# A three-engine attention and Fourier kernel: new chunk order, later values, filter products on GpSimd, one PSUM tile

## The chip, the cores and the metric

The kernel runs on one core of a Trainium2 chip. The metric is the device time of one execution in microseconds, with the median over the runs. Engines are named as the profile names them: PE (TensorE), ACT (ScalarE), DVE (VectorE), POOL (GpSimd), SP (SyncE, which issues DMAs).

## What is computed

The input x has 2048 rows of 448 values. The result is a gated mix of two branches: softmax attention with 16 heads of 28 values, and a spectral filter (a two-dimensional real FFT, a product with a complex weight, and the inverse).

```python
g = sigmoid((x * gate_w).sum(-1, keepdims=True))
qkv = (x @ wqkv) -> q, k, v            # 16 heads of 28
a = softmax(q @ k.T / sqrt(28)) @ v @ wo
X = rfft2(x.astype(float32)) * (w_r + 1j * w_i)
b = irfft2(X, s=(2048, 448)).astype(bfloat16)
return g * a + (1 - g) * b
```

## The kernel before

**Work.** The 16 heads are taken in four groups G of four. A group has four query blocks j of 512 queries; one group and one block make a chunk, 16 in all. A chunk has 16 packs, one for each block of 128 keys, and a pack has four scores tiles of 128 keys x 512 queries, one per head. That is 256 packs.

**Two ways to an exponential.** A pack goes one of two ways. On ACT, two of its score tiles at a time lie side by side in a PSUM tile of two banks and one ACTIVATE (line 862) makes the exponentials of 128 x 1024 scores. On DVE the exponential is put together from integer arithmetic: line 891 turns the scores of one head into bits (128 x 512, out of PSUM), and line 897 makes three shifted copies of the whole pack (128 x 2048, SBUF to SBUF); four variants are then summed by PE. In before 200 packs go to ACT (400 ACTIVATEs) and 56 to DVE (224 of line 891, 168 of line 897).

**PE.** All matmuls are issued from line 913. A score matmul uses 32 rows of the array, so that up to four heads can run side by side. Values (psV) use four tiles of 32 columns side by side; projections and the Fourier matmuls as well (`mmc`, line 915).

**PSUM.** Eight banks of 128 x 512 f32. In before they are six tiles: psA and psB with two banks each for the score tiles of ACT, three tiles psX0 to psX2 of one bank each for everything that DVE evicts (its scores, projections, Fourier steps, output), and psV with one bank for the sum over keys.

```python
self.psS = [ps.tile([128, n, 512], F32, name=f"ps{'AB'[i]}") for i, n in enumerate(sizes)]
self.psX = [ps.tile([128, 512], F32, name=f"psX{i}") for i in range(len(CFG["xbanks"]))]
self.psV = ps.tile([128, 512], F32, name="psV")
```

**Order.** The kernel writes its order of instructions itself. `Plan` (lines 158 to 824) holds an estimated duration for each operation, due times for each piece of side work (`unit(at, name, due)`), and weights (`CFG`, lines 827 to 833). It plays the engines forward and notes in which order every engine takes its work; `build` then emits the instructions in that order, and each engine executes its own list in order. The plan knows banks ("A0", "A1", "B0", "B1", "X0" to "X2", "V") and when each is free. The waits between engines are not the plan's: the framework puts them in when the instructions are emitted, from the tiles that each reads and writes.

**Side work.** Projections of keys and queries (`proj`), of values (`values`, 16 units of 449 columns with all 16 heads and the gate's logit), the forward transform (`fft1`, `fft2`), the product with the filter (line 1384, DVE, out of PSUM), sums of the products on GpSimd (line 1391), the inverse transform (`fft2`, `fft3`), normalising each chunk (`norms`, through small DMAs), and the output (`final`, 16 blocks of 128 rows).

Of the kernel before, what the change touches and what calls it, by code (L numbers as in the profile page):

```python
# [18 lines left out]
FP = F + 1  # L19
# [8 lines left out]
BITS_MIN = 256.0  # L28

# [128 lines left out]
class Plan:  # L158
# [3 lines left out]
    def __init__(self, cfg):  # L162
        self.cfg = cfg
        self.out = []
        self.avail = {e: [] for e in ("ACT", "DVE", "POOL", "SP")}
        self.T = {e: 0.7 for e in ("PE", "ACT", "DVE", "POOL", "SP")}
        self.units = []
        self.ops = []
        self.seq = 0
        self.npend = 0  # L170
# [102 lines left out]
    def run(self):  # L273
# [18 lines left out]
        limit = 1200.0  # L292
        while self.npend > 0 or not self.stream_over():
            eng = min(self.T, key=self.T.get)
            t = self.T[eng]
            if t > limit:
                raise RuntimeError("the plan does not end: " + self.state())
            ok = self.pe_step(t) if eng == "PE" else self.step(eng, t)
            if not ok:
                self.T[eng] = t + 0.02  # L300
# [44 lines left out]
    def setup_stream(self, q_ready, k_ready, v_ready, emit):  # L345
# [14 lines left out]
        self.bank_of = [[f"{'AB'[i]}{k}" for k in range(n)] for i, n in enumerate(self.sizes)]  # L360
        self.last_exp = [None] * len(self.sizes)
# [32 lines left out]
    def operands(self, p):  # L394

        ci, kt = divmod(p, 16)
        a, b = self.q_ready[ci], self.k_ready[ci // 4][kt // 4]
        if a.end is None or b.end is None:
            return None
        return max(a.end, b.end)  # L400
# [9 lines left out]
    def next_tile(self):  # L410
# [7 lines left out]
        while len(units) < size:  # L418
            if cur is None:
# [31 lines left out]
        self.tile = dict(k=k, units=units, ready=ready, slots=slots, grp=k % len(self.sizes))  # L451
        self.ntile += 1
        return self.tile

# [38 lines left out]
    def exp_run(self, e, t):  # L493
# [4 lines left out]
        e["end"] = o.end  # L498
        if not any(self.s_left) and self.last_exp[e["grp"]] is e:
# [5 lines left out]
        for p, h in e["units"]:  # L505
            a = self.act_pack[p]
            a["exps"].append(o)
            if len(a["exps"]) == 4:
                ci, kt = divmod(p, 16)
                x = Op("PE", 0, None, [self.v_ready[ci // 4][kt]] + a["exps"], name="pv")  # L510
# [47 lines left out]
    def d_run(self, d, h, bank, t, conc):  # L558
# [19 lines left out]
        self.s_mark(d["p"] // 64, o.end)  # L578
# [3 lines left out]
    def d_sums(self, d):  # L582
        p = d["p"]
        ci, kt = divmod(p, 16)
        vr = self.v_ready[ci // 4][kt]
# [34 lines left out]
    def pe_step(self, t):  # L620
# [35 lines left out]
        pool = c["xbanks"] if (self.started or self.reserve) and any(self.s_left) else self.allb  # L656
# [67 lines left out]
    def s_run(self, tl, t):  # L724
        self.started = True
        u = Op("PE", 0, None, [], name="s")
# [5 lines left out]
        for b in self.bank_of[tl["grp"]]:  # L732
            self.owner[b] = "stream"
# [4 lines left out]
        for p, h in tl["units"]:  # L738
            G = p // 64
# [5 lines left out]
        fb = self.free_banks(t, self.cfg["xbanks"])  # L745
# [82 lines left out]
    tiles=(2, 2), xbanks=("X0", "X1", "X2"), nring=20, nvar=10, nearly=5, l_pe=0.09, l_act=0.03, pe_lat=0.20,  # L828
    dma_issue=0.6, m_pe=0.2, m_bank=0.1, tol=0.15, max_ahead=9, nd_max=99, d_open=3, ahead=3, d_chunks=1,
    dve_op1=0.605, dve_shift=0.60, pool_shift=2.0, pool_shifts=(), pool_every=0, prio_op1=3, prio_shift=3, sh_max=4, d_urg=0,  # L830
    window=3.413, z_hard=3250, z_soft=3500,
    w_pv=1.0, w_open=0.5, w_new=1.6, w_late=0.5, w_d=3, w_due=2, hungry=1.4, v_rush=0.5, x_rush=4.0, k_rush=5.0, q_rush=0.0, w_hungry=1, sw_pen=0, pv_min=1, ring_urg=2, d_first=True,
# [3 lines left out]
class Emit:  # L836
# [5 lines left out]
    def score(self, p, h, bank):  # L842
        k = self.k
        ci, kt = divmod(p, 16)
        G, j = divmod(ci, 4)
# [3 lines left out]
    def scores(self, tl):  # L849
        for i, (p, h) in enumerate(tl["units"]):  # L850
            self.score(p, h, self.k.pl.bank_ap(f"{'AB'[tl['grp']]}{i}"))

    def exp(self, e):
# [8 lines left out]
        k.nc.scalar.activation(out=out, in_=k.psS[e["grp"]][:, 0:n, :], func=ACT.Exp, scale=LN2_128)  # L862
# [10 lines left out]
    def value(self, p, h, rhs, x):  # L873
        k = self.k
        ci, kt = divmod(p, 16)
        G = ci // 4
# [27 lines left out]
class Kernel:  # L904
# [27 lines left out]
    def tiles(self, ctx):  # L932
# [7 lines left out]
        sizes = CFG["tiles"]  # L940
        self.psS = [ps.tile([128, n, 512], F32, name=f"ps{'AB'[i]}") for i, n in enumerate(sizes)]
        self.psX = [ps.tile([128, 512], F32, name=f"psX{i}") for i in range(len(CFG["xbanks"]))]
# [37 lines left out]
        self.Wo = sb("Wo", [128, NG, D])  # L980
# [4 lines left out]
        self.t12 = [[sb(f"t{n}{i}", [128, 2 * FP]) for n in (1, 2)] for i in range(2)]  # L985
        self.P = sb("P", [128, CFG["nring"], 512])
# [25 lines left out]
    def plan(self):  # L1012
        pl = self.pl = Plan(CFG)
        pl.banks = {}
        for i, n in enumerate(CFG["tiles"]):
            for k in range(n):
                pl.banks[f"{'AB'[i]}{k}"] = self.psS[i][:, k, :]
        for i, b in enumerate(CFG["xbanks"]):
            pl.banks[b] = self.psX[i][:, :]
# [12 lines left out]
        self.group(1, 1.0)  # L1032
        self.gate()
        self.fft2()
        self.group(2, 4.3)
        self.group(3, 8.3)
# [23 lines left out]
    def loads(self):  # L1060
# [10 lines left out]
        self.d_wv = self.dma(self.Wv[0:C, :, 0:D], w3[:, :, 2 * D:3 * D], 9.4, **fast)  # L1071
        self.d_gw = self.dma(self.Wv[0:C, :, D:D + 1], self.gw.rearrange("(c k o) -> k c o", c=NC, o=1), 9.4)
# [21 lines left out]
        self.m_wo = pl.op("POOL", 1.9, lambda e: nc.gpsimd.memset(self.Wo[:, :, :], 0.0), prio=6, port=True)  # L1094
        self.d_wo = []
        wov = self.wo.rearrange("(g h d) n -> h d g n", g=NG, h=4)
        for h in range(4):
            self.d_wo.append(self.dma(self.Wo[32 * h + 1:32 * h + 29, :, :], wov[h], 3.0, [self.m_wo, self.d_bi], prio=7))
# [31 lines left out]
    def square(self, eng, src, i, deps, prio=4, alt=None):  # L1130
# [9 lines left out]
    def head(self):  # L1140
        pl, nc = self.pl, self.nc
        self.o_xT = [[] for _ in range(4)]
        for b in range(4):
            for cp in range(2):
                u = pl.unit(-10, "xT", due=-1, rush=6.0 if b == 0 else CFG["x_rush"])
# [24 lines left out]
        u = pl.unit(-8, "w", due=-1, rush=6.0)  # L1170
# [10 lines left out]
        self.m_wo.deps.append(self.o_wt)  # L1181
        self.queries(0, -6.9945, None, [1, 2, 3], "DVE", deps=[self.o_wt])

    def first(self, which, b, name, sel, one):
# [3 lines left out]
        u = self.proj((-9.5 if b == 0 else -9.0) + 0.1 * b, which, 0, b, name, due=-1, rush=6.0 if b == 0 else CFG["k_rush"])  # L1188
# [13 lines left out]
    def queries(self, G, at, nk, blocks, eng, deps=(), alt=None, span=0.0):  # L1202
# [3 lines left out]
        due = at + 1.5 if G else 0.3  # L1206
# [38 lines left out]
    def group(self, G, at, span=0.18):  # L1245
# [3 lines left out]
        for b in range(4):  # L1249
            u = self.proj(at + span * b, 0, G, b, "k", deps=free, due=at + 1.2)  # L1250
            self.k_ready[G][b] = self.ev_k(u, G, b, deps=free)
            sqs.append(self.square("POOL", self.KT[G % 2][:, 512 * b:512 * b + 512], b, [self.k_ready[G][b], self.sq_use[b]]))
        u = pl.unit(at + span * 4, "kn", due=at + 1.3)
# [12 lines left out]
        u = pl.unit(at + span * 4, "kb", due=at + 1.3)  # L1266
        u.mm(lambda bank: self.mm(bank[:, 0:1], self.mrow4[:, :, :].rearrange("p b h -> p (b h)"), self.one[0:1, 1:2], True, True), n=60, kind="row", deps=[b2])
        nk = u.use("DVE", 0.1, lambda bank, e: nc.vector.tensor_copy(out=self.nks[G % 2][:, :], in_=bank[:, 0:1]), prio=2)
        self.queries(G, at + span * 5, nk, [0, 1, 2, 3], "POOL", deps=free, span=span)


    def values(self):
        nc = self.nc
        self.o_g, evs = [], []
        for t in range(NT):
            u = self.pl.unit(-7 + 0.001 * t, "v", due=(t + 2) / 16, rush=CFG["v_rush"])
            b = t // 4
            for c in range(NC):
                u.mm(lambda bank, c=c, t=t: self.mmc(bank[:, 0:449], self.xT[0:C, c, 128 * t:128 * t + 128], self.Wv[0:C, c, :], c == 0, c == NC - 1),
                     n=449, kind="bg", eff=0.875, deps=self.o_xT[b] + [self.d_wv, self.d_gw])  # L1280

            def ev(bank, e, t=t):
                out = self.Vb[:, t, :, 1:29]
                in_ = bank[:, 0:448].rearrange("p (h d) -> p h d", d=DH)
                nc.scalar.copy(out=out, in_=in_) if e == "ACT" else nc.vector.tensor_copy(out=out, in_=in_)
            o = u.use("DVE", dict(DVE=0.54, ACT=0.5), ev, deps=[self.m_v1], alt="ACT", prio=2)
            evs.append(o)
            for G in range(1, NG):
                self.v_ready[G][t] = o
            self.o_g.append(u.use("DVE", 0.09, lambda bank, e, t=t: nc.vector.tensor_copy(out=self.glog[:, t:t + 1], in_=bank[:, 448:449]), prio=2))  # L1290
        for b in range(4):
# [4 lines left out]
            o = self.pl.op("DVE", dict(DVE=0.54, POOL=1.0), weigh, evs[4 * b:4 * b + 4] + [self.o_wt], prio=0, port=True)  # L1296
            for t in range(4 * b, 4 * b + 4):
                self.v_ready[0][t] = o

    def gate(self):  # L1300
        pl, nc = self.pl, self.nc
        a = pl.op("ACT", 0.12, lambda e: nc.scalar.activation(out=self.ge[:, :], in_=self.glog[:, :], func=ACT.Exp, scale=-1.0), self.o_g)
        a = pl.op("DVE", 0.1, lambda e: nc.vector.tensor_scalar_add(out=self.ge[:, :], in0=self.ge[:, :], scalar1=1.0), [a], port=True)
        a = pl.op("DVE", 0.25, lambda e: nc.vector.reciprocal(out=self.ge[:, :], in_=self.ge[:, :]), [a])
        a = pl.op("DVE", 0.1, lambda e: nc.vector.tensor_copy(out=self.gg[:, 0, :], in_=self.ge[:, :]), [a], port=True)
        a = pl.op("DVE", 0.1, lambda e: nc.vector.tensor_scalar(out=self.gg[:, 1, :], in0=self.gg[:, 0, :], scalar1=-1.0, scalar2=1.0, op0=ALU.mult, op1=ALU.add), [a], port=True)
        u = pl.unit(0.0, "gT", due=0.9)
        u.mm(lambda bank: nc.tensor.transpose(out=bank.bitcast(BF16)[0:32, 0:128], in_=self.gg[:, :, :].rearrange("p a t -> p (a t)"), identity=self.ident), n=128, deps=[a])
        a = u.use("DVE", 0.2, lambda bank, e: nc.vector.tensor_copy(out=self.grow[:, :], in_=bank.bitcast(BF16)[0:32, 0:128]))
        d = self.dma(self.gd[:, :], self.grow[:, :], 2.1, [a])  # L1310
        g = self.gd[:, :]
        self.d_gq = [self.dma(self.gq[32 * h:32 * h + 32, :, :], raw_ap(g, [[16, 32], [512, 4], [1, 16]]), 2.3, [d]) for h in range(4)]
# [46 lines left out]
    def fft2(self):  # L1359
        nc, pl = self.nc, self.pl  # L1360
        loads = [self.load_g(0, [self.d_bd]), self.load_g(1, [self.d_bd])]
        p2use, tuse = [None, None], [[], []]
# [181 lines left out]
```

## Time and profile before

| | us |
|---|---|
| median of 3 runs | 418.14 (417.87 to 425.62) |
| the profiled execution | 417.98 |
| its span | 416.2 |
| first exponential of ACT starts at | 17.39 |
| last one starts at | 399.25 |
| GpSimd busy | 102.4 |

The span is the time from the first to the last instruction that the profile shows; the profiled execution's own time is 1.8 us longer. In a group's row stand the line, the engine, what is written and read, the count, then busy time, the mean duration in ns, and the idle time of the engine ahead of these instructions with what ended it. A timeline row begins with the start and the time it covers, both in us. "PEclk" is the granted clock of TensorE as a share of full speed. A duration in the profile includes the way through the engine: two ACTIVATEs that follow each other without a wait overlap for about 0.1 us.

### The profile page before, as it was taken

How to read it: one execution, taken by the hardware profiler on the slowest of the kernel's cores; microseconds unless marked ns; L12 is line 12 of the kernel's file. 1: busy time of each engine (PE TensorE's matmuls, PEld its weight loads, DVE VectorE, ACT ScalarE, POOL GpSimd, SP SyncE). 2: the span in 40 equal slices, each digit the busy share in tenths (PEclk: the TensorE clock that was granted, in tenths of full speed). 3: DMA queues.
4: the chain of work that ended last, by engine and by line, in shares of the span. 5: the costliest groups of instructions: out<-in, count | busy, mean ns of one | idle time of the engine just before them, and what ended most of it. 6: DMA issues, size and time to landing. Idle time of an engine off the chain costs nothing.

```text
span 416.2 us, 12278 instructions
## 1 busy us (share of the span) xinstructions
PE 394.5 (95%) x5030; PEld 136.2 (33%) x5030; DVE 367.7 (88%) x677; ACT 382.4 (92%) x418; POOL 102.4 (25%) x144
## 2 busy tenths in 40 slices
PE   7999999999999999999999999999999999999993
PEld 4433343222333323323333223223333322223251
DVE  3547699999999999989999899899998999999991
ACT  3895989999999999999999999999999989999941
POOL 0251102652221323331302242251367111010100
PEclk9999999999999999999999999999999989999998
DMA  8520001221022202021121201100100100010203
GB/s 263 151 62 7 4 2 17 53 41 39 11 57 52 84 8 63 4 64 32 37 74 46 58 8 59 39 28 4 28 3 2 28 2 27 4 50 4 70 8 106
DMA packets 23929, 17.66 MB, mean 42 GB/s; under 512 B 15268, under 2 KB 19281, under 8 KB 23873
## 3 DMA queue, kind: packets, MB, share of 16 engines
q1 hardware_dynamic: 22800, 16.59, 14.8%
q8 instruction: 39, 0.64, 0.7%
q10 hardware_dynamic: 1072, 0.29, 0.3%
q14 instruction: 18, 0.14, 0.1%
HBM read 14.71 MB, written 1.97 MB: 40 GB/s over the span
## 4 chain that ended last, share of the span: by engine, by line
PE 42%; ACT 25%; DVE 16%; issue 6%; DMA 6%; SPq 2%; ACTq 0%; DVEq 0%; POOL 0%
ACT P L862 25%; PE psX L913 15%; PE psV L913 13%; PE psB L913 7%; PE psA L913 7%; DVE VS L897 5%; DVE VS L891 5%; DMA rs<-osb 3%; DMA Qf<-in_A_wqkv_dram 2%; SPq L1055 2%; DMA out_dram<-ost 2%; DVE osb L1449 1%; DVE t L1384 1%; DVE tab L1426 1%; DVE QT L1220 0%
## 5 line engine op out<-in xcount | busy, mean ns | idle before, releaser
L862 ACT ACTIVATE P<-psA 128x1024 bf16<-128x1024 f32 x195 | 205.9, 1056 | 7.7 <-PE psV L913 5.4
L862 ACT ACTIVATE P<-psB 128x1024 bf16<-128x1024 f32 x195 | 206.0, 1056 | 3.3 <-PE psB L913 2.1
L891 DVE TENSOR_SCALAR VS<-psX 128x512 int16<-128x512 f32 x224 | 145.4, 680 | 6.1 <-PE psX L913 5.5
L897 DVE TENSOR_SCALAR VS<-VS 128x2048 int16<-128x2048 int16 x168 | 111.1, 714 | 0.4
L913 PEld LDWEIGHTS <-KT 32*128 32x128 bf16 (+1 forms) x1040 | 46.0, 91 | 144.4 <-issue 141.4
L913 PE MATMUL psV<-VS,Vb 128*32 128x512 bf16 x916 | 82.2, 389 | 2.0 <-DVE VS L897 1.7
L913 PE MATMUL psB<-QT,KT 32*128 32x512 bf16 x400 | 78.4, 384 | 5.9 <-ACT P L862 5.0
L913 PE MATMUL psA<-QT,KT 32*128 32x512 bf16 x400 | 79.7, 384 | 1.1 <-ACT P L862 0.6
L913 PE MATMUL psV<-P,Vb 128*32 128x512 bf16 x780 | 74.6, 386 | 0.0
L913 PE MATMUL psX<-QT,KT 32*128 32x512 bf16 x224 | 73.1, 384 | 1.3 <-DVE VS L891 0.6
L913 PEld LDWEIGHTS <-Vb 128*32 128x32 bf16 x1696 | 36.7, 94 | 64.8 <-issue 59.1
L1391 POOL TENSOR_TENSOR t<-t,t 128x226 bf16<-128x226 bf16 x32 | 19.1, 618 | 59.2 <-DVE t L1384 49.9
L1137 POOL TENSOR_TENSOR sq<-QT 128x512 bf16<-128x512 bf16 x16 | 17.1, 1071 | 59.9 <-DVE QT L1220 33.5
L1458 POOL TENSOR_TENSOR xtok<-osb,RB 128x512 bf16<-128x512 f32 x12 | 15.8, 1318 | 39.8 <-DMA RB<-rgd 39.8
L1432 POOL TENSOR_TENSOR UZ<-tab 128x225 bf16<-128x225 f32 (+1 forms) x32 | 19.4, 632 | 17.8 <-DMA RB<-rgd 9.5
L1137 POOL TENSOR_TENSOR sq<-KT 128x512 bf16<-128x512 bf16 x12 | 12.9, 1072 | 39.5 <-DVE KT L1127 38.8
L913 PE MATMUL psX<-xT,Wq 112*32 112x512 bf16 x240 | 19.6, 383 | 0.2 <-DVE VS L891 0.2
L913 PE MATMUL psX<-xT,Wk 112*32 112x512 bf16 x240 | 19.8, 384 | 0.0
L913 PE MATMUL psX<-Bd,UZ 112*32 112x452 bf16 x256 | 19.1, 358 | 0.0
L1384 DVE TENSOR_TENSOR t<-psX,Wf 128x452 bf16<-128x452 f32 x32 | 18.9, 617 | 0.0
L1458 POOL TENSOR_TENSOR xT<-osb,RB 128x512 bf16<-128x512 f32 x3 | 4.4, 1454 | 56.2 <-DMA RB<-rgd 56.2
L913 PE MATMUL psX<-Wv,xT 112*32 112x449 bf16 x240 | 16.0, 357 | 0.0
(111 smaller groups left out, 307.0 us busy)
## 6 DMA issues: line engine op xcount, KB each, us to landing
tab<-c_tab SPq DMA_DIRECT2D x16, 256.0 KB
RB<-rgd SPq DMA_DIRECT2D x60, 64.0 KB
xtok<-in_A_x_dram SPq DMA_DIRECT2D x4, 448.0 KB
out_dram<-ost SPq DMA_DIRECT2D x6, 224.0 KB
rs<-osb SPq DMA_DIRECT2D x60, 2.0 KB
Wf<-in_B_w_r_dram SPq DMA_DIRECT2D x31, 28.1 KB
Wf<-in_B_w_i_dram SPq DMA_DIRECT2D x31, 28.1 KB
Qf<-in_A_wqkv_dram SPq DMA_DIRECT2D x2, 294.0 KB
```

The source lines that it names most:

```text
L862: k.nc.scalar.activation(out=out, in_=k.psS[e["grp"]][:, 0:n, :], func=ACT.Exp, scale=LN2_128)
L891: k.nc.vector.tensor_scalar(out=k.VS[:, slot, 512 * h:512 * h + 512], in0=bank, scalar1=float(BITS0), scalar2=BITS_MIN, op0=ALU.add, op1=A ...
L897: k.nc.vector.tensor_scalar(out=k.VS[:, dst, :], in0=k.VS[:, src, :], scalar1=float(SHIFTS[v - 1]), scalar2=None, op0=ALU.add)
L913: self.nc.tensor.matmul(out, lhsT=lhsT, rhs=rhs, start=start, stop=stop, skip_group_check=True, **kw)
L1055: (self.nc.sync if e == "SP" else self.nc.scalar).dma_start(out=out, in_=in_)
L1137: (self.nc.vector if e == "DVE" else self.nc.gpsimd).tensor_tensor(out=sq[:, :], in0=src, in1=src, op=ALU.mult)
L1384: ts.append(u.use("DVE", 0.55, lambda bank, e, i=i, q=q: nc.vector.tensor_tensor(out=self.t12[i][q][:, :].rearrange("p (r f) -> p r f", r= ...
L1391: (nc.vector if e == "DVE" else nc.gpsimd).tensor_tensor(out=t1[:, FP * q:FP * q + FP], in0=t1[:, FP * q:FP * q + FP], in1=t2[:, FP - FP * ...
L1426: c = u.use("DVE", 0.54, lambda bank, e, eo=eo: nc.vector.tensor_copy(out=eo, in_=bank[:, 0:450]), deps=self.i1_last + use[t % 2])
L1432: nc.gpsimd.tensor_tensor(out=z, in0=a, in1=b, op=ALU.subtract if q else ALU.add)
L1449: ev = pl.op("DVE", 0.61, lambda e: nc.vector.tensor_copy(out=self.osb[:, :], in_=self.psV[:, :]), [pl.pv_done[ci], prev], prio=0, name="e ...
L1458: prev = pl.op("POOL", 1.3, lambda e, G=G, j=j: nc.gpsimd.tensor_tensor(out=self.ON[G][:, 512 * j:512 * j + 512], in0=self.osb[:, :], in1= ...
```

## The change

- The chunks are taken in another order: groups 2 and 3 alternate (`CHUNKS`), so that the last chunks are (2,2), (3,2), (2,3), (3,3).
- The values are projected in two parts: group 0 with the gate's logit at once (four units of 4 x 113 columns), groups 1 to 3 later (16 units of 336 columns, `v2`).
- The product with the filter leaves DVE: DVE copies the transform out of PSUM into FX (f32), and GpSimd makes the two products.
- Psum: psA, psB and the three psX become one tile psS of seven banks, in which the banks' places are X0 A0 A1 X1 B0 B1 X2. New functions of the plan (`widen`, `one_more`, `apart`) can make a score tile wider by a neighbouring bank, up to `widest` banks; `widest` is 2 and a tile has 2.
- The plan's weights can differ from chunk to chunk (`seg`), due times and priorities are changed. The plan now gives 201 packs to ACT (402 ACTIVATEs) and 55 to DVE (220 and 165).
- The output weights Wo take the place of the forward table Bd after its last use; the last four output blocks have buffers of their own (sq) instead of turns in ost; the output blocks are due earlier.

```diff
+BANKS = {(2, 2): "X0 A0 A1 X1 B0 B1 X2", (3, 2): "A0 A1 A2 X0 B0 B1 X1", (3, 3): "A0 A1 A2 X0 B0 B1 B2", (2, 1): "X0 A0 A1 X1 B0 X2 X3"}
+CHUNKS = [(0, j) for j in range(4)] + [(1, j) for j in range(4)] + [(2, 0), (2, 1), (3, 0), (3, 1), (2, 2), (3, 2), (2, 3), (3, 3)]
...
+    def widen(self, tl, t):
+        fb = self.free_banks(t, self.xbanks)
...
+        for b in sorted((lo, hi), key=lambda b: b == "X1"):
+            if b not in fb or len(fb) <= keep or len(tl["units"]) >= c["widest"]:
+                continue
+            if not self.one_more(tl, t):
+                return
...
-        self.psS = [ps.tile([128, n, 512], F32, name=f"ps{'AB'[i]}") for i, n in enumerate(sizes)]
-        self.psX = [ps.tile([128, 512], F32, name=f"psX{i}") for i in range(len(CFG["xbanks"]))]
+        self.psS = ps.tile([128, 7, 512], F32, name="psS")
+        self.place = {b: i for i, b in enumerate(BANKS[CFG["tiles"]].split())}
...
-        for i, n in enumerate(CFG["tiles"]):
-            for k in range(n):
-                pl.banks[f"{'AB'[i]}{k}"] = self.psS[i][:, k, :]
-        for i, b in enumerate(CFG["xbanks"]):
-            pl.banks[b] = self.psX[i][:, :]
+        for b in sorted(self.place):
+            pl.banks[b] = self.psS[:, self.place[b], :]
...
-        k.nc.scalar.activation(out=out, in_=k.psS[e["grp"]][:, 0:n, :], func=ACT.Exp, scale=LN2_128)
+        k.nc.scalar.activation(out=out, in_=k.psS[:, k.place[e["banks"][0]]:k.place[e["banks"][0]] + n, :], func=ACT.Exp, scale=LN2_128)
...
+        for b in range(4):
+            u = self.pl.unit(-0.1 + 0.001 * b, "v", due=0.1 + b / 4, rush=CFG["v_rush"])
...
         for t in range(NT):
-            u = self.pl.unit(-7 + 0.001 * t, "v", due=(t + 2) / 16, rush=CFG["v_rush"])
+            u = self.pl.unit(CFG["v2_at"] + 0.11 * t, "v2", due=CFG["v2_due"] + 0.05 * t)
...
+            fx = u.use("DVE", 0.55, lambda bank, e, i=i: nc.vector.tensor_copy(out=self.FX[i][:, :], in_=bank[:, 0:452]), deps=fuse[i])
             ts = []
             for q in range(2):
-                ts.append(u.use("DVE", 0.55, lambda bank, e, i=i, q=q: nc.vector.tensor_tensor(
-                    out=self.t12[i][q][:, :].rearrange("p (r f) -> p r f", r=2), in0=bank[:, 0:452].rearrange("p (r f) -> p r f", r=2),
+                ts.append(pl.op("POOL", 1.2, lambda e, i=i, q=q: nc.gpsimd.tensor_tensor(
+                    out=self.t12[i][q][:, :].rearrange("p (r f) -> p r f", r=2), in0=self.FX[i][:, :].rearrange("p (r f) -> p r f", r=2),
...
-            u = pl.unit(13.0 + j + 0.25 * (t % 4) - (0.6 if j == 3 else 0.0) if j < 3 else 16.5, "out")
+            at = (12.6, 13.2, 14.3, 15.99)[j] + (0.15 if j < 3 else 0.001) * (t % 4)
+            u = pl.unit(at, "out", due=at + 0.5 if j < 3 else 99.0)
...
-                out = self.ost[:, t % 4, :]
+                out = self.ost[:, t % 4, :] if t < 12 else self.sq[t % 4][:, 0:D]
```

## The prediction

> **What bounds the kernel now.** I read the page first (totals, costliest groups), then ScalarE's timeline (how often an exp starts), then the chain of waits and the timeline of the end, then stretches around the one place where the clock fell, and last the order of both built programs, engine by engine, with the waits and the addresses in each instruction. Page and timelines:
>
> ```profile
> span 416.2 us, 12278 instructions
> PE 394.5 (95%) x5030; PEld 136.2 (33%) x5030; DVE 367.7 (88%) x677; ACT 382.4 (92%) x418; POOL 102.4 (25%) x144
> L862 ACT ACTIVATE P<-psA 128x1024 bf16<-128x1024 f32 x195 | 205.9, 1056 | 7.7 <-PE psV L913 5.4
> L891 DVE TENSOR_SCALAR VS<-psX 128x512 int16<-128x512 f32 x224 | 145.4, 680 | 6.1 <-PE psX L913 5.5
> ...
> 35.55 1.14 ACT L862 ACTIVATE P<-psB 128x1024 bf16<-128x1024 f32 x1
> 40.98 1.02 ACT L862 ACTIVATE P<-psA 128x1024 bf16<-128x1024 f32 x1 [4.29 <-PE psV L913]
> 41.91 1.02 ACT L862 ACTIVATE P<-psB 128x1024 bf16<-128x1024 f32 x1
> 42.81 1.03 ACT L862 ACTIVATE P<-psA 128x1024 bf16<-128x1024 f32 x1
> 43.71 1.04 ACT L862 ACTIVATE P<-psB 128x1024 bf16<-128x1024 f32 x1
> ```
>
> Three engines are nearly full at the same time, and that is what the time rests on. An exp lasts 1.03 us, but the next begins 0.90 us after it, because its scores lie ready in the other tile: psA fills while psB is read. From the first exp (17.39 us) to the start of the last (399.25 us) there are 399 steps: 399 x 0.905 = 361.1 us of steady stream, and 20.8 us of stalls. With 17.4 us ahead and 16.9 us from the last exp's start to the end this is the span. ScalarE's stream bounds the kernel, and it holds only while PE writes one PSUM tile, ScalarE reads a second and VectorE a third, all at once.
>
> **What matters in the change.** The tiles psA, psB and three psX (7 banks) become one tile psS of 7 banks. I looked at how the program orders accesses to one PSUM tile. The end of before shows it:
>
> ```profile
> 404.73 9.21 SPq L1055 DMA_DIRECT2D out_dram<-ost  x7
> 409.31 1.16 DVE L1490 CAST ost<-psB 128x448 bf16<-128x448 f32 x2 [3.54 <-DMA out_dram<-ost]
> 410.51 0.37 PE L913 MATMUL psB<-UZ,R1s 128*32 128x448 bf16 x4 [2.67 <-DVE ost L1490]
> ```
>
> By the program's addresses the first of the two casts reads psB's second bank and the second its first bank; the matmuls then write the second bank. That bank was read by about 409.9 (a cast of this shape takes 0.60). The matmul waited for the other bank's cast (409.31 + 1.16 = 410.47) and started at 410.51. So a whole tile is ordered here, not a bank.
>
> In the program of after this holds everywhere. I counted the accesses to psS in program order: 3464 matmuls, 416 by ScalarE, 384 by VectorE. The engine changes 1348 times, and 1347 times the next one waits for the last access of the one before it, reads against reads too: ScalarE waits for VectorE 284 times (9 in before), VectorE for ScalarE 270 times (8 in before). An exp on banks 4 and 5 waits for the filter's copy out of bank 6; scores for one tile wait for the exp on the other. So the three engines take turns on psS, and the time is the sum of the turns, no longer the fullest engine.
>
> **The sum of the turns.**
> - ScalarE: 402 exps (two more than before, since 55 packs instead of 56 go to VectorE) x 1.03 = 414; 14 other reads (4 copies x 1.01, 5 squares x 0.60, 4 casts x 0.535, one 0.45) = 10. Together 424 us.
> - VectorE: 291 reads of 512 columns (220 of them the score bits, 0.68; those with a bias 0.74) = 199; 63 of 448 to 452 columns x 0.615 = 39; 16 of 336 columns, a shape not in before, between 0.285 (128 columns) and 0.615 (450), by width 0.49 = 8; small ones 5. Together 250 us.
> - PE: 552 turns with 1189 passes (up to four matmuls side by side), 463.7 thousand columns. At full clock 512 columns take 0.213, so 193 us + 5 of pass overhead; a turn ends only when its last result has landed, 0.39 - 0.22 = 0.17 later, x 552 = 94; 252 changes between row and column tiles within a turn x 0.12 = 30. Together 322 us. At half clock the columns cost 386 and the turn's end 0.62 - 0.42 = 0.20 or less: about 520 us.
> - Handovers: after ScalarE or VectorE PE starts 0.05 later (409.31 + 1.16 to 410.51), ScalarE 0.10 after PE (22 idle gaps, 0.04 to 0.12), VectorE 0.06. ScalarE against VectorE has no such row; the nearest bound it by 0 and 0.12, and I take each engine's own figure. 327 + 224 into PE, 257 + 158 into ScalarE, 295 + 87 into VectorE: 29 + 42 + 23 = 93 us.
>
> Work off psS hides: 429 value passes on psV lie ahead of PE's turns (0.4 us each at half clock, in the 1 to 2 us that the others take), and I compared turn by turn: under 5 us stick out. The 165 shifts (0.60 apart) fit between VectorE's turns, over 3 us apart on average. If that cover were gone they would cost 165 x 0.60 = 99 us.
>
> Outside the turns: 5.2 us to the first transpose, some 5 for the last values and the 20 small steps that normalise the last chunk (3.0 us in before, now one block after another), 2.7 from the last cast to the end: 13 us.
>
> **Which clock.** Half, and the trace has the case:
>
> ```profile
> core 0: us, PE busy (x) PEld busy (x) DVE busy (x) ACT busy (x) POOL busy (x), PEclk, DMA share, GB/s
> 215.10:218.50 3.40, 2.83 (x37) 0.97 (x26) 3.40 (x7) 3.40 (x5) 0.00 (x0) 1.00 0.03 8
> 334.60:338.00 3.40, 2.74 (x23) 0.70 (x24) 3.40 (x7) 3.40 (x5) 0.00 (x0) 1.00 0.00 0
> 338.00:341.40 3.40, 3.34 (x26) 0.64 (x25) 3.29 (x7) 2.28 (x3) 0.00 (x0) 0.50 0.05 7
> ...
> 337.48 0.39 PE L913 MATMUL psB<-QT,KT 32*128 32x512 bf16 x2 [0.53 <-ACT P L862]
> 339.04 0.61 PE L913 MATMUL psA<-QT,KT 32*128 32x512 bf16 x2
> ```
>
> After 3.4 us with 23 matmuls the granted clock fell to 0.50 for 3.4 us, and a score tile took 0.61 instead of 0.39; after 37 matmuls it stayed at 1.00. After has 5258 matmuls. Spread over 1100 us that is 16 in 3.4 us, over 1300 us 14: below 23 either way. The Trainium skill ("TensorE: Matmul & The Clock Gate", HAM oscillation) asks only that PE have no idle gap over about 3.4 us; by that rule the PE term would be 322 (the second rival), and the trace disagrees with it at 334.60.
>
> Half clock: 424 + 250 + 520 + 93 + 13 = 1300 us. A few dense stretches at the start may run at full clock; for 5% of PE's 200 us of difference I take off 10: span 1290. The measured time of this profiled execution is 417.98, 1.8 over its span and within 0.2 of the median 418.14; I predict 1290, the 1.8 being below what I can resolve.
>
> **The other edits**, all within the sum and small:
> - Filter products: 32 VectorE reads of psX (0.617) become 16 copies (0.615 for 450 columns) in f32, 9.9 us less reading. GpSimd gets 32 products: by its rows (1.07 for 512 bf16, 1.32 with f32, 1.53 with a broadcast) 1.0 to 1.35 each, 31 to 43 us on an engine idle for three quarters. Their waiters, the inverse transforms, follow much later.
> - Values: the same columns (64 x 113 + 64 x 336 = 64 x 449), 20 evictions for 16. It takes away what stalled ScalarE after 35.55 us in before (4.5 + 0.3 + 1.3 = 6.1 us), which the turns no longer show.
> - Chunk order, due times, later Wo load (four loads behind one 1.6 us memset, on queues with slack), own output buffers for the last four blocks: no new work. The last ends ScalarE's wait of 9.55 us for out_dram<-ost.
>
> **The rivals.**
> 1. *Banks ordered apart: faster.* Had the waits the bank's extent, or cost nothing because what they name is always done, ScalarE would bound again: 17.4 + 401 x 0.905 = 362.9, stalls 20.8 - 6.1 = 14.7, and an end of about 10 (16.9 less the 6.8 by which the last cast comes sooner without the DMA wait) = 405, measured 407. It decides from the point where a wait names an access that ended before the scores are ready. For it: psA and psB in before do alternate freely. Against it: 410.47 to 410.51, and that each wait names the access just before. The skill's "PSUM — Partial Sum Buffer" (PSUM bank collisions) says the chip needs order only by bank and quadrant; by that rule 407 would come out. No wait of after follows it. Chance 0.05.
> 2. *Full clock: 1100.* The turns add up (424 + 250 + 322 + 93 + 13 = 1102), but the clock stays at 1.00, because what counts for it is PE's longest idle gap and not its work: no gap here comes near 3.4 us. For it: after 26 matmuls at half clock it came back at 341.4. Against it: it fell with PE busy for 2.74 of 3.40 us, and 14 to 16 matmuls are fewer still. Chance 0.13.
> 3. *Dearer turns: over 1400.* If each handover cost 0.18 instead of 0.07, since many instructions wait for two or three semaphores, 1348 x 0.11 = 148 us more: 1440. The rows of ScalarE's gaps end at 0.12. Chance 0.04.
>
> **How the numbers follow.** Main case 0.78, its own range 1200 to 1390 (handovers 0 to 0.12 for the pairs without a row, -15 to +10; turn's end 0.10 to 0.25 x 552, -55 to +30; clock partly full, -50; small waits of values on the evacuation of psV, 15 chunks x up to 2 us, +30). To leave out no more than 2 in 10 the range must reach the full clock: 1090 to 1400. About 2% is what a measurement of this kernel can tell from no change (417.87 to 425.62). Faster 0.05 (rival 1), within 2% 0.01, slower 0.94.
>
> **What would show it.** Right: no two of ScalarE's exps less than 1.03 us apart, ScalarE idle before most of them, released by DVE or PE in turn; all engines' busy shares far down (ACT about 33%); PEclk at 5 in most slices; score matmuls of 0.6 us. Wrong clock: PEclk 9 and a span near 1100. Wrong altogether: exps 0.90 us apart.

## The result and the profile after

The changed kernel takes 1290.42 us (median of 4 runs, 1289.24 to 1290.94). The kernel before took 418.01 beside it (417.87 to 425.62). The ratio is 3.087, with a 95% interval of 3.081 to 3.093. Ratios here leave out runs that were disturbed by a low clock; the medians given for repeated runs take them in.

The first rows of the page of after, and then its costliest groups (line, engine, operation, what is written and read, count; busy us and mean ns of one; idle time ahead and what ended most of it):

```profile
span 1287.5 us, 12827 instructions
PE 721.0 (56%) x5258; PEld 195.3 (15%) x5258; DVE 388.5 (30%) x647; ACT 422.5 (33%) x419; POOL 133.4 (10%) x176
PEclk6555555555555555555555555555555555555556
...
L970 ACT ACTIVATE P<-psS 128x1024 bf16<-128x1024 f32 x392 | 401.1, 1023 | 809.7 <-PE psS L1021 463.1
L1021 PE MATMUL psS<-QT,KT 32*128 32x512 bf16 x1024 | 269.1, 596 | 313.2 <-ACT P L970 149.8
L999 DVE TENSOR_SCALAR VS<-psS 128x512 int16<-128x512 f32 x220 | 152.1, 692 | 459.5 <-PE psS L1021 334.5
```

Before, the three engines were busy for 95, 92 and 88% of a short span; now for 56, 33 and 30% of a long one. ScalarE's and VectorE's work is nearly the same in us (382 and 368 before, 423 and 389 now; ScalarE's 40 more are about what 400 exps gain when each no longer overlaps the next by 0.1 us). What is new is the idle time: ScalarE stood for 810 us ahead of its exps, 7.7 us ahead of half of them before. PE's clock row shows half speed nearly throughout. (A slice is 32 us; a 6 needs more than 6 us of it at full speed, so three single stretches of 3.4 us at full speed don't show in the row.)

ScalarE's timeline of after from 500 us on (start and time covered in us; in brackets the idle time before and what ended it):

```profile
502.07 1.02 ACT L970 ACTIVATE P<-psS 128x1024 bf16<-128x1024 f32 x1 [2.83 <-DVE VS L999]
505.15 1.02 ACT L970 ACTIVATE P<-psS 128x1024 bf16<-128x1024 f32 x1 [2.05 <-DVE Qf L1519]
509.62 1.02 ACT L970 ACTIVATE P<-psS 128x1024 bf16<-128x1024 f32 x1 [3.45 <-PE psS L1021]
511.96 1.02 ACT L970 ACTIVATE P<-psS 128x1024 bf16<-128x1024 f32 x1 [1.32 <-PE psS L1021]
```

The same stretch with all engines, around the second of these exps:

```profile
504.42 0.69 DVE L1519 CAST Qf<-psS 113x512 bf16<-113x512 f32 x1 [2.44 <-PE psS L1021]
505.15 1.02 ACT L970 ACTIVATE P<-psS 128x1024 bf16<-128x1024 f32 x1 [2.05 <-DVE Qf L1519]
...
506.20 0.69 DVE L999 TENSOR_SCALAR VS<-psS 128x512 int16<-128x512 f32 x1 [1.09 <-ACT P L970]
...
506.95 0.61 PE L1021 MATMUL psS<-QT,KT 32*128 32x512 bf16 x3 [1.67 <-DVE VS L999]
```

The second block is read by adding start and duration: 504.42 + 0.69 = 505.11, and ScalarE starts at 505.15; 505.15 + 1.02 = 506.17, and VectorE starts at 506.20; 506.20 + 0.69 = 506.89, and PE starts at 506.95. Each instruction begins when the one before it on psS is through, whichever engine that was and whichever bank it read. Exps start 3.1 us apart (median; the nearest two 1.72), where before it was 0.905. The view of waits sums this up (line that waited, for what: us of idle time, times, longest; L970 is the exp, L999 VectorE's bits of the scores, L1021 the matmuls):

```profile
ACT P L970 <- PE psS L1021: 463.1, 236, 3.5
...
PE psS L1021 <- ACT P L970: 318.0, 288, 1.9
...
ACT P L970 <- DVE VS L999: 225.8, 100, 4.5
...
PE psS L1021 <- DVE VS L999: 125.4, 120, 2.6
DVE VS L999 <- ACT P L970: 124.9, 54, 5.4
```

The third and the last of these lines are the ones to look for: an exp and a bits instruction exchange no data, and each waits for the other more than 50 times, once for over 4 us.

### The profile page after: what moved, and what is told of

It is laid out like the page before. It is cut to its first block, busy times and chain, and to the rows that moved or that the text cites. A ratio compares the mean times of both kernels' runs of the same rounds, so it can differ in the third digit from the quotient of the medians.

```text
span 1287.5 us, 12827 instructions
## 1 busy us (share of the span) xinstructions
PE 721.0 (56%) x5258; PEld 195.3 (15%) x5258; DVE 388.5 (30%) x647; ACT 422.5 (33%) x419; POOL 133.4 (10%) x176
## 4 chain that ended last, share of the span: by engine, by line
PE 41%; ACT 32%; DVE 20%; issue 5%; DMA 1%; DVEq 0%; ACTq 0%; SPq 0%
PE psS L1021 39%; ACT P L970 31%; DVE VS L999 12%; PE psV L1021 1%; DVE Qf L1519 1%; DVE P L1482 1%; DVE tab L1542 1%; ACT VS L970 1%; DVE UZ L1446 1%; DVE FX L1491 1%; DVE KT L1228 1%; DVE QT L1319 1%; DVE Vb L1394 1%; DVE ost L1607 1%; DMA Qf<-in_A_wqkv_dram 0%
## 5 line engine op out<-in xcount | busy, mean ns | idle before, releaser
L970 ACT ACTIVATE P<-psS 128x1024 bf16<-128x1024 f32 x392 | 401.1, 1023 | 809.7 <-PE psS L1021 463.1
L1021 PE MATMUL psS<-QT,KT 32*128 32x512 bf16 x1024 | 269.1, 596 | 313.2 <-ACT P L970 149.8
L999 DVE TENSOR_SCALAR VS<-psS 128x512 int16<-128x512 f32 x220 | 152.1, 692 | 459.5 <-PE psS L1021 334.5
L1021 PEld LDWEIGHTS <-KT 32*128 32x128 bf16 (+1 forms) x1040 | 70.0, 99 | 545.1 <-issue 542.8
L1021 PE MATMUL psV<-VS,Vb 128*32 128x512 bf16 x900 | 128.7, 618 | 0.0
L1021 PE MATMUL psV<-P,Vb 128*32 128x512 bf16 x784 | 117.7, 616 | 0.0
L1021 PE MATMUL psS<-xT,Wq 112*32 112x512 bf16 x256 | 38.6, 606 | 47.3 <-ACT P L970 34.3
L1494 POOL TENSOR_TENSOR t<-FX,Wf 128x452 bf16<-128x452 f32 x32 | 33.0, 1049 | 287.9 <-DVE FX L1491 277.6
L1021 PE MATMUL psS<-xT,Wk 112*32 112x512 bf16 x256 | 37.4, 608 | 41.6 <-ACT P L970 26.2
L1021 PE MATMUL psS<-Bd,UZ 112*32 112x452 bf16 x256 | 35.3, 559 | 39.8 <-ACT P L970 32.4
L1021 PEld LDWEIGHTS <-Vb 128*32 128x32 bf16 x1684 | 39.7, 111 | 114.0 <-issue 113.5
L1021 PE MATMUL psS<-Wv,xT 112*32 112x336 bf16 (+1 forms) x448 | 33.3, 393 | 40.7 <-ACT P L970 27.7
L1021 PE MATMUL psS<-Bi,Qf 113*32 113x225 bf16 x256 | 19.8, 377 | 30.1 <-ACT P L970 18.6
L1548 POOL TENSOR_TENSOR UZ<-tab 128x225 bf16<-128x225 f32 (+1 forms) x32 | 20.3, 658 | 149.3 <-DVE tab L1542 149.3
L1021 PEld LDWEIGHTS <-xT 112*32 112x32 bf16 (+1 forms) x576 | 17.6, 120 | 76.0 <-issue 74.4
L1021 PE MATMUL psS<-tab,t 128*32 128x256 bf16 (+1 forms) x256 | 19.4, 406 | 15.8 <-ACT P L970 13.5
```

Of the source, the lines that this page charges most:

```text
L970: k.nc.scalar.activation(out=out, in_=k.psS[:, k.place[e["banks"][0]]:k.place[e["banks"][0]] + n, :], func=ACT.Exp, scale=LN2_128)
L999: k.nc.vector.tensor_scalar(out=k.VS[:, slot, 512 * h:512 * h + 512], in0=bank, scalar1=float(BITS0), scalar2=BITS_MIN, op0=ALU.add, op1=A ...
L1021: self.nc.tensor.matmul(out, lhsT=lhsT, rhs=rhs, start=start, stop=stop, skip_group_check=True, **kw)
L1494: ts.append(pl.op("POOL", 1.2, lambda e, i=i, q=q: nc.gpsimd.tensor_tensor(out=self.t12[i][q][:, :].rearrange("p (r f) -> p r f", r=2), in ...
L1548: nc.gpsimd.tensor_tensor(out=z, in0=a, in1=b, op=ALU.subtract if q else ALU.add)
```

## The experiments

The theory: one tile is ordered as a whole, so the engines take turns, and the clock halves since PE does too little work in 3.4 us. The diffs show how the tiles are made; the exps and the table of banks are pointed at the new tiles to match. The rivals: another part of the change is the cause; the clock goes by something else than work; a part of the tile would do the same.

**The tile cut apart again in after** (e1), with all other edits, and the instructions and their order as in after:

```diff
-        self.psS = ps.tile([128, 7, 512], F32, name="psS")
+        self.psA = ps.tile([128, 2, 512], F32, name="psA")
+        self.psB = ps.tile([128, 2, 512], F32, name="psB")
+        self.psX = [ps.tile([128, 512], F32, name=f"psX{i}") for i in range(3)]
...
-            pl.banks[b] = self.psS[:, self.place[b], :]
+            pl.banks[b] = self.psX[int(b[1])][:, :] if b[0] == "X" else (self.psA, self.psB)[b[0] == "B"][:, int(b[1]), :]
```

> The changed kernel with psS cut back into psA, psB and three psX; every instruction and its order stay. Theory (only the shared tile costs): 872 us go, ScalarE bounds again with exps 0.905 apart, PEclk 1.00, and the price of the first rival holds: 407 us, 400 to 414, faster than before by 1% to 4%. Rival (the rest of the change costs too, for instance GpSimd's products late or the new chunk order): 418 or more.

Measured: 413.19 us (412.87 to 419.47), ratio to before 0.9868 (0.9795 to 0.9941). From its page:

```profile
span 411.1 us, 12740 instructions
PE 392.5 (95%) x5258; PEld 135.6 (33%) x5258; DVE 367.9 (90%) x647; ACT 385.9 (94%) x419; POOL 139.5 (34%) x176
...
L970 ACT ACTIVATE P<-psB 128x1024 bf16<-128x1024 f32 x196 | 205.5, 1048 | 3.7 <-PE psB L1021 1.9
L970 ACT ACTIVATE P<-psA 128x1024 bf16<-128x1024 f32 x196 | 205.3, 1047 | 5.8 <-PE psA L1021 4.3
```

And ScalarE's timeline of e1 at the place where ScalarE stood still for 4.3 us in before:

```profile
40.09 1.02 ACT L970 ACTIVATE P<-psA 128x1024 bf16<-128x1024 f32 x1
41.01 1.02 ACT L970 ACTIVATE P<-psB 128x1024 bf16<-128x1024 f32 x1
41.91 1.03 ACT L970 ACTIVATE P<-psA 128x1024 bf16<-128x1024 f32 x1
```

The number of tiles alone is worth 877 us: the idle time ahead of the exps went from 810 us to under 10, and starts are again 0.9 us apart. It is also faster than before, by 1.3% here.

**One tile in before, and nothing else** (e2):

```diff
-        self.psS = [ps.tile([128, n, 512], F32, name=f"ps{'AB'[i]}") for i, n in enumerate(sizes)]
-        self.psX = [ps.tile([128, 512], F32, name=f"psX{i}") for i in range(len(CFG["xbanks"]))]
+        one = ps.tile([128, 7, 512], F32, name="psS")
+        self.psS = [one[:, 1:3, :], one[:, 4:6, :]]
+        self.psX = [one[:, i, :] for i in (0, 3, 6)]
```

> The kernel before with its five score and work tiles made one tile of seven banks; nothing else. Theory (turns on one tile): 1374 handovers x 0.068 = 93, ScalarE 420, VectorE about 270 (32 products read PSUM here), PE 507 at half clock, ends 8: 1300 us, 1270 to 1330, clock near 0.51. Rival (the turns need the new order or the plan's new weights to hurt): well under 1000.

Measured: 1295.48 us in one run, span 1293.7, clock 0.51. From its page:

```profile
PEclk6555555555555555555555555555555555555557
...
L862 ACT ACTIVATE P<-psS 128x1024 bf16<-128x1024 f32 x390 | 399.4, 1024 | 810.6 <-PE psS L913 442.1
```

Removing the merge takes the whole loss away (e1), and the merge alone brings it all back. The other edits have no part in the loss.

**Two smaller merges in after.** In e4 psA and psB are one tile of four banks and the psX stay apart; in e5 the three psX are one tile and psA and psB stay apart. Their edits against after, e4 first:

```diff
-        self.psS = ps.tile([128, 7, 512], F32, name="psS")
+        self.psS = ps.tile([128, 4, 512], F32, name="psS")
+        self.psX = [ps.tile([128, 512], F32, name=f"psX{i}") for i in range(3)]
```

```diff
-        self.psS = ps.tile([128, 7, 512], F32, name="psS")
+        self.psA = ps.tile([128, 2, 512], F32, name="psA")
+        self.psB = ps.tile([128, 2, 512], F32, name="psB")
+        self.psX = ps.tile([128, 3, 512], F32, name="psX")
```

> The changed kernel with psA and psB as one tile of four banks and three psX apart. Theory (turns): VectorE leaves the chain, PE and ScalarE alternate: 402 x (1.02 + 0.05 + 0.10 + a score pass of 0.39 at full or 0.60 at half clock) = 627 or 712, with 25 us ahead and behind 650 to 740; the work per 3.4 us is near the edge where the clock fell, so both clocks are open. Rival (the reads of ScalarE and VectorE against each other make most of the loss): near 420.

> The changed kernel with psA and psB apart and only the three psX as one tile. Theory (turns): PE and VectorE alternate on psX, 600 handovers x 0.06 = 36; VectorE's reads 250; PE's 299 turns with 316 thousand columns 132 at full clock + 51 for the turns' ends + 12 = 195: a chain of 481, longer than ScalarE's 386, so 500 to 560 us with the ends and PE's score and value passes between; at 520 us the work per 3.4 us is above the edge, clock 0.9 or more. Rival (only ScalarE's part in the turns matters, since it was the bound): near 413.

Measured: 751.32 us (e4, clock 0.555), above its range, and 693.79 us (e5, clock 0.674), far above its range of 500 to 560. From the timeline of e4:

```profile
401.02 1.02 ACT L970 ACTIVATE P<-psS 128x1024 bf16<-128x1024 f32 x1 [0.92 <-PE psX L1021]
...
402.10 0.61 PE L1021 MATMUL psS<-QT,KT 32*128 32x512 bf16 x2 [0.20 <-ACT P L970]
...
402.80 1.02 ACT L970 ACTIVATE P<-psS 128x1024 bf16<-128x1024 f32 x1 [0.75 <-PE psX L1021]
...
403.87 0.61 PE L1021 MATMUL psS<-QT,KT 32*128 32x512 bf16 x2 [0.19 <-ACT P L970]
```

Only ScalarE and PE take turns here, at half clock: 0.61 for the scores, 0.10, 1.02 for the exp, 0.05, so 1.78 us for each of 402 exps, 716 us. (The releaser named at 402.80 is a score matmul for VectorE that ran beside ScalarE's and ended with it; the exp reads what the matmul of 402.10 wrote by 402.71.) A turn is the time from the first to the last access of one engine in a row, a handover the time from its end to the next engine's start. The turns on psS add up: ScalarE 413.7, PE 241.3, handovers 79.1, VectorE 0.8, and 14.7 at both ends are the span of 749.5. What took e4 above its range were mainly the handovers, for which 402 x 0.15 = 60 us had been expected. In e5 the turns add up too (PE 342.8, VectorE 247.3, ScalarE 7.5, handovers 86.2, ends 8.2: 692.0). My miss was PE's term (195 expected), for which I had taken a nearly full clock, and after it the handovers (36 expected). The clock was at half in most of the span, and 565 matmuls on other tiles (scores and values) fell inside PE's turns on psX; how PE's excess divides between the two is not shown. A merge is expensive even where only two engines share the tile, or where the tile holds only side work.

**More work for PE.** Both kernels are after with four zero passes on psV for each score tile; in e3 ahead of the scores, in e6 right behind each exp in PE's order, where PE waits for it anyhow (from the 17th). In e3 zero passes fall between the projections of group 0's values, which are made on psV (54.9 to 59.6 us), so e3 probably leaves out some of these values; its time alone is read here. e3's edit, then e6's:

```diff
     def scores(self, tl):
+        for _ in range(4):
+            self.zero("col", None, False)
```

```diff
         k.nc.scalar.activation(out=out, in_=k.psS[:, k.place[e["banks"][0]]:k.place[e["banks"][0]] + n, :], func=ACT.Exp, scale=LN2_128)
+        if e["k"] >= 16:
+            for _ in range(4):
+                self.zero("col", None, False)
```

> The changed kernel with four more passes of zeros on psV (each 512 columns, adding zero) ahead of each of the 402 score tiles: 1608 passes more work for PE. Theory (the clock goes by PE's work in 3.4 us): the work per 3.4 us rises from 14 matmuls to about 34, the clock comes to 1.00, PE's turns fall from 512 to about 322 us, the zeros lie in the other engines' turns: 1100 to 1150 us, faster than the changed kernel by more work. Rival (the clock is held down by something else, such as the many short rests): clock stays near 0.5, the zeros (1.7 us each time) stick out behind ScalarE's 1.03 us: over 1350.

> The changed kernel with four passes of zeros on psV after each exp from the 17th on, instead of ahead of each score tile: now they lie in ScalarE's turn (1.02 us; four passes take 0.85 at full clock) and not inside PE's. Theory (clock by work in 3.4 us, edge near 3000 columns of the whole array): about 4200 per 3.4 us, clock above 0.9, PE's turns near 330 instead of 512, time 1100 to 1170: more matmuls, less time. Rival (the extra passes always cost more than the clock gives, as in the run with them ahead of the scores): above 1290.

Measured: 1427.01 us (e3) and 1149.39 us (e6). The clock row of e3's page:

```profile
PEclk6758977976789879768786886788766689798997
```

The clock row of e6's page and its score matmuls:

```profile
PEclk6559998999989999999998999988999888998999
...
L1024 PE MATMUL psS<-QT,KT 32*128 32x512 bf16 x1024 | 183.2, 406 | 171.8 <-DVE VS L1002 61.6
```

e6 does more work than after and is 141 us faster: PE's turns on psS went from 512.2 to 355.2 us, since the mean clock rose from 0.511 to 0.918 and a score matmul lasts 406 ns instead of 596. Work for PE raises the clock, with every wait of after in place. e3 says the same of the clock (0.789) but missed its 1100 to 1150 us, and its timeline shows why:

```profile
602.10 0.62 PE L1023 MATMUL psS<-xT,Wq 112*32 112x512 bf16 x4 [0.62 <-ACT P L972]
602.48 1.94 PE L1023 MATMUL psV<-cst 128*32 128x512 bf16 x16
604.36 0.61 PE L1023 MATMUL psS<-QT,KT 32*128 32x512 bf16 x2
```

The sixteen zero matmuls lie between two pieces of work on psS, so they are part of PE's turn, and the other engines wait 1.9 us for them. PE's turns grew to 591.8 us and the handovers to 149.6. So e3's time is in its rival's range and its clock is not: the added work raised the clock, and cost more in the turns than it paid.

**What the other edits bring, with the tiles apart.** In e7 and again in e11, e1's filter products are back on VectorE, out of PSUM (the plan then gives ScalarE 406 exps instead of 402). In e8 the edits at the end (due times, own output buffers, priorities of the last steps) are put into before alone. e10 is e1 once more, beside e11 on one chip.

```diff
-            fx = u.use("DVE", 0.55, lambda bank, e, i=i: nc.vector.tensor_copy(out=self.FX[i][:, :], in_=bank[:, 0:452]), deps=fuse[i])
...
-                ts.append(pl.op("POOL", 1.2, lambda e, i=i, q=q: nc.gpsimd.tensor_tensor(
+                ts.append(u.use("DVE", 0.55, lambda bank, e, i=i, q=q: nc.vector.tensor_tensor(
```

e8's edit against before (its main part; priorities of the last steps change as well):

```diff
-            u = pl.unit(13.0 + j + 0.25 * (t % 4) - (0.6 if j == 3 else 0.0) if j < 3 else 16.5, "out")
+            at = (12.6, 13.2, 14.3, 15.99)[j] + (0.15 if j < 3 else 0.001) * (t % 4)
+            u = pl.unit(at, "out", due=at + 0.5 if j < 3 else 99.0)
...
-                out = self.ost[:, t % 4, :]
+                out = self.ost[:, t % 4, :] if t < 12 else self.sq[t % 4][:, 0:D]
```

> The changed kernel with the tiles apart, and the filter products back on VectorE (32 reads of PSUM, no FX copies). The plan gives 203 packs to ACT instead of 201. Theory (ScalarE bounds, products on GpSimd save VectorE 16 x 0.6 = 10 us, which is two packs): 4 more exps x 0.905 = 3.6 us more than the 413.2 with products on GpSimd, 415 to 419. Rival (GpSimd's products hold VectorE's shifts up as much as they save): 411 to 414.

> The kernel before with only the end of the change: due times of the output blocks, own buffers (sq) for the last four, and the last chunk's blocks normalised one after another. 402 exps by its plan. Theory (with the tiles apart, the end is all that the change gains: 16.9 us from the last exp's start to the end became 9.3, and two exps more cost 1.8): 411 to 414, like the changed kernel with the tiles apart. Rival (the later values gain as well, 6.1 us at 35 us): 417 or more here would mean that the end needs the other parts; under 410 that they only cost.

> The split version unchanged, to be compared with the next kernel on the same chip. Theory (the other edits gain some 4 to 5 us, mostly at the end): median 412 to 415, ratio to before 0.985 to 0.993. Rival (the gain of the first look was luck with the clock): the interval holds 1.000.

> The split version with the filter products back on VectorE, beside the split version on the same chip. Theory: the products on GpSimd take 9.9 us off a VectorE that is 88 to 90% busy, and this shows as 2 to 5 us: median 415 to 419, and fewer ACTIVATEs could not make up for it. Rival: VectorE's reads are not what ScalarE waits for; then the fastest runs of both kernels differ by less than 1 us and only the half-clock stretches differ.

| | median (all runs) | ratio to before |
|---|---|---|
| e7, products on VectorE | 418.23 (413.29 to 428.02) | 0.9958 (0.9914 to 1.0003) |
| e8, before with the end edits | 422.52 (415.78 to 422.77) | none given |
| e10, e1 again | 414.31 (412.65 to 425.69) | 0.9909 (0.9873 to 0.9944) |
| e11, e7 again | 415.90 (412.03 to 425.54) | 0.9943 (0.9907 to 0.9978) |

e1's gain holds when it is repeated (e10): about 1%. In e1's trace the last exp starts at 401.77 (399.25 before, with two exps fewer) and the end behind it takes 9.3 us instead of 16.9, so it is the end that brings it; the stall of 4.3 us is gone, but as much came back in small stalls from 137 us on (22.1 us of stalls altogether, 21.0 before; a stall is what a step from one exp's start to the next has over 0.905 us). Where the filter products are better done is not settled: e10's and e11's intervals overlap, e11's median lies in its theory's range, and its fastest run of 412.03 beside e10's 412.65 is what its rival asked for. e8 missed its 411 to 414: in the profiled run its end is shorter (11.4 us), but its stream lost 28 us instead of 21, in part around two stretches of half clock (at 221.7 and 327.5 us). Its fastest run took 415.78 and the fastest of before beside it 416.15, so what the end edits bring by themselves is not shown.

**More zero passes where the tiles are apart** (e9). Runs of one kernel differ by 6 to 15 us here, and I took half-clock stretches for the cause. The plan has a weight for the least work in 3.413 us, raised here and for six single chunks (there to 3750):

```diff
-    sh_max=4, d_urg=2, window=3.413, z_hard=3250, z_soft=3500, v2_at=2.0, v2_due=2.8, g_at=(0.9, 4.3, 8.0), g_due=1.0, w_pv=1.0, w_open=0.5,
+    sh_max=4, d_urg=2, window=3.413, z_hard=3650, z_soft=3900, v2_at=2.0, v2_due=2.8, g_at=(0.9, 4.3, 8.0), g_due=1.0, w_pv=1.0, w_open=0.5,
```

> The split version again, with the plan told to keep more work on PE in every 3.413 us (its least work 3650 to 3750 where it was 3250 to 3550), which it does with zero passes on psV. Theory: the spread between runs of the split kernels (412.9 to 419.5, and 413.3 to 428.0 with the products on VectorE) comes from single stretches of 3.4 us at half clock, after windows whose work falls below about 3000; with more work no such stretch is left. Then the clock is 0.998 or more in the profiled run, the slowest run lies within 3 us of the fastest, and the median is at 412 to 416. Rival: PE is busy for 95% of the span, so the added passes push score tiles back; then the clock is as high but every run is slower, the fastest above 417.

Measured: 420.07 us (416.47 to 426.88), ratio 1.0026 (0.9988 to 1.0064). The theory missed: the spread is as wide as ever, the clock of single runs went from 0.971 to 1.000, and in the profiled run one window held work of only 1536. So the work that the plan counts in its windows is not what the chip saw in its own. The rival has half a point: all runs are slower than e1's fastest (its sign, a fastest run above 417, was missed by little), but what the trace shows is a reordered plan (406 exps instead of 402, an end of 12.0 us instead of 9.3) and not score tiles pushed back (22.1 us of stalls in both).

## Why the prediction was right, by its steps

1. *A whole tile is ordered, not a bank.* Shown by e1 and e2 in both directions. The first rival (banks apart, 407) fell: the waits of after name the access just before, at 505.15, 506.20 and 506.95. Its price was near the truth for a kernel in which banks really are apart: e1 took 413.2 and 414.3. I had reckoned with 14.7 us of stalls, and there were 22.1, the gain at 35 us having come back later.
2. *The time is the sum of the turns.* The 1348 handovers are there, and in none does an engine start before the one ahead is through. So the terms, added up in the trace from the starts and ends of the accesses to psS, are the span:

| us | predicted | measured |
|---|---|---|
| ScalarE's turns | 424 | 420.8 |
| VectorE's turns | 250 | 254.9 |
| PE's turns, at half clock | 520 | 512.2 |
| handovers | 93 | 91.7 |
| ends | 13 | 7.8 |
| off for full-clock stretches | -10 | (in PE's term) |
| span | 1290 | 1287.5 |

   The handovers without a row of their own were the guess in it. ScalarE hands over to VectorE in 0.04 us on average and VectorE to ScalarE in 0.06, less than the 0.06 and 0.10 I took, and PE to VectorE in 0.10 instead of 0.06. The two errors cancel: predicted 23 + 42 into VectorE and ScalarE, measured 32 + 30. That the whole sum comes within 3 us of the span is in part luck too: single terms are off by up to 5 us, in both directions.
3. *Half the clock.* The granted clock was 0.50 from 11.8 us on, but for three windows of 3.4 us and the last ones; after held 13.6 matmuls in 3.4 us (401 from 600 to 700 us), predicted 14. The second rival (only an idle gap counts, 1100) fell: PE's longest time without a matmul in after is 2.65 us, and yet the clock stayed at half for up to 860 us on end. That is against the rule of the Trainium skill ("TensorE: Matmul & The Clock Gate", HAM oscillation) as I put it. The rival's price is near where the clock does rise: e6, with a clock of 0.918, took 1149.
4. *Dearer turns.* No: the mean handover was 0.068 us, the rival's 0.18. What the rival named is there, only smaller: the 74 handovers from VectorE to ScalarE in which an instruction of ScalarE that does nothing but wait (EVENT_SEMAPHORE) stands right ahead of the exp or copy took 93 ns, the other 84 took 33 (medians).
5. *The small edits.* GpSimd's products took 1.05 us each, 33.0 us in all, of a predicted 31 to 43. The new evictions of 336 columns took 0.51 each, predicted 0.49. That both hide, as argued, fits e1, where they cost nothing that shows; for the products e11 leaves it open, and no run takes the new evictions out alone.

What the prediction did not treat is the spread between runs when the tiles are apart, in before as well (415.18 to 427.01 us in 24 runs). It didn't matter for a ratio of 3.09, but it is wider than all that the rest of the change brings.

## What to carry to other kernels

Before two PSUM tiles are made one, count how often the engine changes in the accesses to the new tile, in program order, since the framework here orders a whole tile, reads against reads too: where the tile holds the main work, the time becomes the sum of the turns, whatever banks are touched. A plan that knows banks doesn't help when the tiles given to the framework are coarser than what it plans with; keep one tile for each set of banks that is to be free on its own. And where engines start to take turns, look at PE's work in each 3.4 us as well: in four kernels here with merged tiles and no added work (after, e2, e4, e5) the mean clock fell to between 0.51 and 0.67.

## What the runs showed of the hardware

**The clock goes by weighted work in free-running windows.** In all traces the granted clock changes on a grid of 3.41 us. I counted for each window the columns of the matmuls that started in it, each weighted with the share of the 128 x 128 array that it uses (a quarter for most shapes here); by an estimate from passes of 512 columns that start 0.216 us apart at full clock in before, a window full of whole-array matmuls would have some 8100. In some 2700 windows of 13 profiles (before, after and eleven experiments), every window below 2560 was followed by half clock, every one above 3488 by full clock, and between them both occur. Between them the clock of the window itself goes along with what follows: half clock followed 260 of 344 windows at half clock, but 68 of 206 at full. Whether the clock holds on to its state there, or counting a matmul wholly in the window in which it starts makes it look so, is open. Before fell after 2816 at 334.6 us; in after the median window held 1408. PE's busy time tells much less than the weighted work: the best edge puts 695 windows on the wrong side instead of 85. The Trainium skill ("TensorE: Matmul & The Clock Gate", Part 1: The HAM clock gate) gives a free-running window of 3413 ns, and the traces agree; that some matmuls run in every window isn't enough, they show besides.

**Where the grid lies can decide whether a thin stretch costs anything.** One pair of traces shows it. e1 and e10 are one kernel, and up to 21 us after the start their matmuls run within 0.07 us of each other. In e1 the grid's windows from 20.3 and 23.7 us on held 4268 and 4016, and the clock stayed at 1.00. In e10 the window from 21.3 us on held 2462; the clock was at 0.50 for the next 17 us, and the matmul that started at 36.6 us in e1 started 7.4 us later in e10. In 24 runs of before on one chip the time goes with the mean granted clock: 415.18 us at 1.000 and 427.01 at 0.964, with a correlation of -0.95 and 3.3 us for each 0.01. One window at half clock lowers the mean by 0.004, so by this slope it costs an estimated 1.3 us, and three of them about as much as e1 gains.

**Handovers go with the waits that an engine has to carry.** In after, from the end of one engine's access to the start of the next one's: into PE 51 ns from ScalarE and 53 from VectorE (medians of 327 and 224). Into ScalarE and VectorE there are two groups. Where no EVENT_SEMAPHORE instruction stands right ahead of the access, it took 33 to 34 ns between ScalarE and VectorE, either way (80 handovers to VectorE, 84 to ScalarE), and 37 to 38 from PE (16 and 99); where one does, 93 ns from VectorE to ScalarE (74), 101 from ScalarE to VectorE (7), 96 from PE to ScalarE (241, of which 106 took under 70) and 115 from PE to VectorE (196, all medians). e2 shows the same groups (33 and 93 from VectorE to ScalarE, 76 and 81 handovers).
